# Start and late batches of a one-core Sinkhorn attention and FFN kernel: exps of two heads merged in the first batch, P of the first pair spread on its own, fillers only in idle banks, two planner costs changed

## The chip, the cores and the metric

The kernel runs on one core of a Trainium2 chip. The metric is the device time of one execution in microseconds (us). Before the change the median of three runs was 229.92 us (229.88 to 229.97). Most executions of a kernel agree within 0.3%. Each execution also reports the mean clock that TensorE was granted (1.0 is full speed). Runs well above the fastest of the same kernel are called slow and kept out of every comparison.

## The reference

```python
def _attn_ref(q, k, v, sort_net):            # B=4, H=8, S=768, D=64, 8 blocks of 96
    P = sort_net                             # [4, 8, 8, 8]
    for _ in range(5):                       # Sinkhorn
        P = np.exp(P - P.max(-1, keepdims=True))
        P = P / (P.sum(-1, keepdims=True) + 1e-09)
        P = P / (P.sum(-2, keepdims=True) + 1e-09)
    k_sorted = einsum('bhij,bhjcd->bhicd', P, k_b)   # blocks of k and v mixed by P
    v_sorted = einsum('bhij,bhjcd->bhicd', P, v_b)
    scores = scale * q_b @ k_sorted^T        # within each block of 96
    return softmax(scores) @ v_sorted

def _moe_ref(x, w_in, w_out):                # x [3072, 512], w_in [512, 2048], w_out [2048, 512]
    h = np.maximum(x @ w_in, 0.0)
    return h * h @ w_out                     # of the attention's result, reshaped to tokens
```

The FFN is most of the work. Its first 384 tokens need the first half of batch 0's attention, and everything before that is start-up.

## The kernel before

The order of instructions on each engine is fixed by a small list scheduler in Python. Every stage is entered with an estimated cost in us and the stages that it depends on. The scheduler fills TensorE (PE) with attention stages that are due and otherwise with FFN work.

```python
FIRST = ("K0 V0 k1 v1 S0 t0 S1 k2 V2 t1 A0 S2 K3 t2 A1 V3 X0 A2 S3 t3 x1 A3 X2 x3")
```

This is the order of the first half of batch 0. The digit is the unit (a pair of heads). K and V sort k and v with P. S makes the scores and their exp. T transposes the sorted v. A multiplies exp by v and divides by the row sums. X transposes the result for the FFN. A capital means that ScalarE copies the result out of PSUM, a small letter that VectorE does.

Buffers rotate in rings: `ps1` has one PSUM bank (transposes of v and of the result share it), `p2` has two tiles of two banks (scores and A), `psf` has three banks. Before the FFN starts, gaps that the plan foresees on PE are filled with matmuls on a tile of ones, all into `p2[0]`, so that PE stays busy:

```python
    def fill(us, wide=False):
        if wide:
            ...      # int(us / 0.33) matmuls of 512 columns into p2[0]
        else:
            for _ in range(int(us / 0.08)):
                nc.tensor.matmul(out=p2[0][:, 1, 384:512], lhsT=ones, rhs=ones,
                                 start=True, stop=True)
...
    for op in plan.run():
        if op.eng == "PE":
            started = started or op in plan.ffn
            if filled and not started and op.gap > 0.15:
                fill(op.gap, op.begin < 11 and op.gap > 0.5)
            filled = True
        op.fn(op.eng)
```

P comes out of the Sinkhorn steps, is transposed (`pT`), and is spread over the partitions by eight matmuls for all heads at once. VectorE multiplies it with a mask for the first two heads, and ScalarE copies it for the others:

```python
    pe = plan.add("PE", 0.3, p_spread, [op] + old)
    w0 = build_w(0, 2, None, pe)                  # VectorE reads pt_ps
    cp = plan.add("ACT", 0.37, ... copy(out=pt, in_=tiles["pt"]), [pe])   # ScalarE reads pt_ps
    rf.use(sf, pe, w0, cp)
```

The exps of one half of a unit are two instructions, one for each head, which also permute the queries:

```python
            for h in range(2):
                def ex(e, h=h, st=st, et=et_r[u.et[hf]]):
                    nc.scalar.activation(
                        out=et[:, h, 0:HS].rearrange("p (n c a) -> p n c a", c=C0, a=NA),
                        in_=st["p"][0:96, h, 0:HS].rearrange("p (n a c) -> p n c a", c=C0, a=NA),
                        func=AF.Exp, scale=scale)
```

In batches 2 and 3 the sort is done by small matmuls from `kb` and `vb` (function `s_nat`, entered with a PE cost of 0.2). `kn` and `qi` are copied into natural order and transposed by DMA into `kx` and `qT`. Scores are entered with a cost of 0.17 in every batch. An FFN unit of 384 tokens has 16 groups of four `hp` matmuls (0.65 us each), then 48 `op` matmuls.

The softmax here doesn't subtract the row's maximum and nothing guards it: scores larger than these inputs give would overflow.

## Time and profile before

| | before |
|---|---|
| time, us | 229.92 |
| span in the profile, us | 228.1 |
| PE busy, us (share) | 220.0 (96%) |
| P transposed on PE (`pT` starts), us | 11.56 |
| last A of the first half starts, us | 21.41 |
| first FFN matmul, us | 23.68 |
| `wtp`, the first stage of batch 2's attention on PE, us | 83.86 |
| start of the last block of 64 `hp` matmuls, us | 203.47 |

Read it from the end. The last block of `hp` and what follows have no gaps, so the time is decided by when that block starts. The stretch from 23.7 to 83.9 us is dense FFN and attention of batches 0 and 1. What can be moved is the start (0 to 23.7) and holes between 84 and 203.

The page's chain of the work that ended last, before the change, as shares of the span by engine:

```profile
PE 81%; ACT 6%; DVE 6%; DMA 4%; issue 2%; POOL 0%; ACTq 0%; DVEq 0%; POOLq 0%
```

PE holds 81% of the chain. The 12% of ScalarE (ACT) and VectorE (DVE), 27 us, are not all waits of PE: PE is idle for only 228.1 - 220.0 = 8.1 us of the span. Four more lines of the very beginning are used below (the timeline: start us, duration us, engine, line, operation; x is the count; in brackets the idle time before it and what ended it):

```profile
5.30 0.96 PE L338 MATMUL p<-ones 128*128 128x512 bf16 x2
6.73 0.76 PE L458 MATMUL qtp<-ident,qb 64*64 64x64 bf16 x36 [0.46 <-DMA qb<-in_q_dram]
...
1.49 1.52 POOL L253 DMA_DIRECT2D qb<-in_q_dram  x2
...
3.11 0.37 DVE L322 TENSOR_TENSOR p_sb<-p_sb,rs 32x64 f32<-32x64 f32 x1
```

### The profile page before, as it was taken

What the parts mean: (1) busy time and instruction counts of PE and PEld (TensorE: products, weight loads), DVE (VectorE), ACT (ScalarE), POOL (GpSimd) and SP (SyncE); (2) the same over time, 40 slices, a digit from 0 to 9 for tenths busy, and PEclk for the clock granted to TensorE, in tenths of its full rate; (3) what the DMA queues carried; (4) which work ended last, traced back from release to release, by engine and by line L of the source; (5) the groups of instructions that cost most, each with busy time, mean ns of one, the idle gap of its engine ahead of it and who ended that gap; (6) DMA issues with size and microseconds to landing.
All of it is one profiled execution on the core that took longest, in us unless ns stands there. A gap on an engine that the chain in (4) does not pass through costs nothing.

```text
span 228.1 us, 5299 instructions
## 1 busy us (share of the span) xinstructions
PE 220.0 (96%) x2152; PEld 125.2 (55%) x2165; DVE 106.0 (46%) x295; ACT 122.3 (54%) x260; POOL 27.1 (12%) x49
## 2 busy tenths in 40 slices
PE   8998999999999999999999999999999999999993
PEld 2576666546665645535665455445665455446552
DVE  5777677407676416630667027523664045005300
ACT  4655676317875328734866248535774177137421
POOL 8963322200003200000000000000000000000000
PEclk9999999999999999999999999999999999999999
DMA  5999999999922999599821341998732210110012
GB/s 60 201 203 207 207 207 204 203 223 249 195 50 26 122 238 205 131 156 265 188 37 35 83 126 25 164 226 196 98 53 53 92 47 3 46 55 37 0 49 92
DMA packets 42744, 28.83 MB, mean 126 GB/s; under 512 B 22752, under 2 KB 38368, under 8 KB 42720
## 3 DMA queue, kind: packets, MB, share of 16 engines
q0 software_dynamic: 13888, 13.63, 37.4%
q1 hardware_dynamic: 28832, 14.86, 30.0%
q8 instruction: 17, 0.28, 0.5%
q14 instruction: 7, 0.06, 0.1%
HBM read 28.89 MB, written 7.91 MB: 161 GB/s over the span
## 4 chain that ended last, share of the span: by engine, by line
PE 81%; ACT 6%; DVE 6%; DMA 4%; issue 2%; POOL 0%; ACTq 0%; DVEq 0%; POOLq 0%
PE op L823 34%; PE hp L795 30%; PE p L544 3%; DVE ao L727 3%; PE p L716 3%; ACT h L803 2%; ACT et L567 2%; DMA qb<-in_q_dram 2%; PE p L503 2%; PE qtp L458 2%; PE op L857 2%; PE vbp L583 1%; PE p L617 1%; DMA qT<-qi 1%; PE p L343 1%
## 5 line engine op out<-in xcount | busy, mean ns | idle before, releaser
L795 PE MATMUL hp<-xT,w_in_bf 128*128 128x384 bf16 x512 | 91.0, 326 | 0.0
L823 PE MATMUL op<-w_out_bf,h 128*128 128x512 bf16 x355 | 82.4, 379 | 0.7
L803 ACT ACTIVATE h<-hp 128x384 bf16<-128x384 f32 x128 | 61.5, 497 | 24.1 <-PE hp L795 19.3
L806 DVE TENSOR_TENSOR h<-h 128x384 bf16<-128x384 bf16 x128 | 44.2, 355 | 53.2 <-ACT h L803 52.4
L795 PEld LDWEIGHTS <-w_in_bf 128*128 128x128 bf16 x512 | 47.1, 98 | 30.1 <-issue 0.7
L823 PEld LDWEIGHTS <-h 128*128 128x128 bf16 x368 | 34.9, 98 | 39.7 <-issue 0.7
L184 ACT COPY ob<-op 128x512 f32<-128x512 f32 (+1 forms) x25 | 14.2, 569 | 56.8 <-PE op L823 54.3
L567 ACT ACTIVATE et<-p 96x384 bf16<-96x384 f32 x64 | 26.2, 489 | 5.5 <-PE p L544 5.5
L727 DVE TENSOR_TENSOR ao<-p,rec 96x512 bf16<-96x512 f32 x32 | 22.0, 687 | 1.1
L726 DVE RECIPROCAL rec<-p 96x8 f32<-96x8 f32 x32 | 6.4, 199 | 21.4 <-PE p L716 18.7
L716 PEld LDWEIGHTS <-et 96*128 96x128 bf16 x256 | 10.7, 97 | 2.9 <-issue 0.3
L253 POOL DMA_DIRECT2D qb<-in_q_dram x8 | 6.0, 755 | 32.8 <-PE qtp L458 25.6
L186 DVE COPY vs<-vbp 96x512 bf16<-96x512 bf16 (+1 forms) x12 | 6.1, 509 | 7.1 <-PE vbp L583 6.9
L253 POOL DMA_DIRECT2D vb<-in_v_dram x10 | 6.6, 659 | 6.4 <-DMA w_in_bf<-in_moe_w_in_dram 3.6
L253 POOL DMA_DIRECT2D kb<-in_k_dram x10 | 6.6, 659 | 6.2 <-DMA w_in_bf<-in_moe_w_in_dram 1.8
L184 ACT CAST ksT<-p 128x768 bf16<-128x768 f32 (+1 forms) x7 | 4.6, 663 | 3.3 <-PE p L503 3.3
L544 PEld LDWEIGHTS <-kx 64*128 64x128 bf16 x128 | 4.6, 155 | 2.8 <-issue 2.8
L716 PE MATMUL p<-vs,et 96*128 96x65 bf16 x128 | 6.0, 193 | 0.0
L716 PE MATMUL p<-vblk,et 96*128 96x65 bf16 x128 | 5.6, 193 | 0.1
L458 PEld LDWEIGHTS <-qb 64*64 64x64 bf16 (+1 forms) x144 | 3.5, 109 | 3.9 <-issue 1.9
L583 PE MATMUL vbp<-ident,vsT 128*128 128x128 bf16 x64 | 5.6, 220 | 0.0
L544 PE MATMUL p<-qT,kx 64*128 64x96 bf16 x128 | 5.6, 226 | 0.0
(81 smaller groups left out, 132.0 us busy)
## 6 DMA issues: line engine op xcount, KB each, us to landing
out_dram<-ob SPq DMA_DIRECT2D x23, 256.0 KB, 2.6
qb<-in_q_dram POOLq DMA_DIRECT2D x8, 384.0 KB, 16.7
vb<-in_v_dram POOLq DMA_DIRECT2D x6, 384.0 KB, 17.1
kb<-in_k_dram POOLq DMA_DIRECT2D x6, 384.0 KB, 17.0
w_in_bf<-in_moe_w_in_dram POOLq DMA_DIRECT2D x4, 512.0 KB, 12.4
w_out_bf<-in_moe_w_out_dram POOLq DMA_DIRECT2D x4, 512.0 KB, 17.7
v_way<-vn SPq DMA_DIRECT2D x4, 396.0 KB, 3.9
vblk<-v_way SPq DMA_DIRECT2D x4, 396.0 KB, 4.0
```

What stands on the lines that cost most here:

```text
L184: nc.scalar.copy(out=out, in_=in_)
L253: nc.gpsimd.dma_start(out=dst, in_=src)
L458: nc.tensor.transpose(out=t["p"][64 * h:64 * (h + 1), a, :], in_=qb[p0:p1, 2 * hp + h, D * a:D * (a + 1)], identity=ident[p0:p1, p0:p1])
L544: nc.tensor.matmul(out=scp[:, h, BLK * n:BLK * (n + 1)], lhsT=(u.ksT[64 * h:64 * (h + 1), hf, BLK * n:BLK * n + 128] if u.b < 2 else kx_r[ ...
L567: nc.scalar.activation(out=et[:, h, 0:HS].rearrange("p (n c a) -> p n c a", c=C0, a=NA), in_=st["p"][0:96, h, 0:HS].rearrange("p (n a c) - ...
L583: nc.tensor.transpose(out=vbp[:, n, :], in_=u.vsT[:, i // NQ, BLK * (i % NQ):BLK * (i % NQ) + 128], identity=ident)
L716: nc.tensor.matmul(out=oup[:, h, 66 * n:66 * n + D + 1], lhsT=et_r[u.et[hf]][:, h, BLK * n:BLK * n + 128], rhs=(u.vs[:, NQ * hf + n, h, 0: ...
L727: nc.vector.tensor_tensor(out=u.ao[:, n0:n0 + NQ, :, :].rearrange("p n e d -> p e n d"), in0=ov[:, :, :, 0:D], in1=rec[:, :, :, None].to_b ...
L795: nc.tensor.matmul(out=t["hp", nt][:, 0:HS], lhsT=w_in_bf[:, kc, 128 * nt:128 * (nt + 1)], rhs=xT[:, kc, t0:t0 + HS], start=(kc == 0), sto ...
L803: nc.scalar.activation(out=t["h1", nt], in_=t["hp", nt][:, 0:HS], func=AF.Relu)
L806: nc.vector.tensor_tensor(out=t["h2"][:, nt, :], in0=t["h1", nt], in1=t["h1", nt], op=ALU.mult)
L823: nc.tensor.matmul(out=t["op", mt], lhsT=t["h2"][:, nt, 128 * mt:128 * (mt + 1)], rhs=w_out_bf[:, nt, :], start=(nt == 0), stop=(nt == NT ...
```

## The change

The intent: the start of batch 0 waits for small copies and exps, so give P to the first pair sooner, merge two exps into one, move copies to the engine that has time, and keep filler matmuls out of banks that someone still reads. The diff also edits two planner costs.

```diff
-FIRST = ("K0 V0 k1 v1 S0 t0 S1 k2 V2 t1 A0 S2 K3 t2 A1 V3 X0 A2 S3 t3 x1 A3 X2 x3")
+FIRST = ("K0 V0 K1 v1 S0 t0 S1 k2 t1 A0 V2 S2 K3 t2 A1 V3 X0 A2 S3 t3 x1 A3 X2 x3")
...
+    def idle(self, t0, t1):
+        for slot, ops in enumerate(self.all):
+            if all(op.end <= t0 or op.begin >= t1 for op in ops):
+                return slot
...
-        nc.gpsimd.memset(kx[:, 128 * NA:], 0.0)
+        nc.vector.memset(kx[:, 128 * NA:], 0.0)
...
-    def fill(us, wide=False):
+    def fill(us, slot):          # into p2[slot]; wide matmuls wherever us > 0.5
...
-            out=pick, in_=ident.rearrange("p (j c) -> p j c", c=C0)[:, :, 0:4]), [cp])
+            out=pick, in_=ident.rearrange("p (j c) -> p j c", c=C0)[:, :, 0:4]), [x_done[0, HP - 1, 0]])
...
         def ev(e):               # qT of batch 0 is stored in natural order
+            if b == 0:
+                copy(e, qT.rearrange("p (i c a) -> p i c a", a=NA, c=C0)
+                     [:, p0 // C0:p1 // C0, :, :], src.rearrange("p a (i c) -> p i c a", c=C0))
...
-            pe = plan.add("PE", 0.17, mm, [u.k_op, u.q_op] + old, due, mode="row")
+            pe = plan.add("PE", 0.17 if u.b < 2 else 0.26, mm, [u.k_op, u.q_op] + old, due,
+                          mode="row")
...
+            if u.b == 0:
+                def ex(e, st=st, et=et_r[u.et[hf]]):
+                    nc.scalar.activation(out=et[:, :, 0:HS], in_=st["p"][0:96, :, 0:HS],
+                                         func=AF.Exp, scale=scale)
...
-            pe = plan.add("PE", 0.2, mm, [landed[b, t, HP * g, 0], built["t"]] + old, due,
+            pe = plan.add("PE", 0.15, mm, [landed[b, t, HP * g, 0], built["t"]] + old, due,
...
-    pe = plan.add("PE", 0.3, p_spread, [op] + old)
+    pe = plan.add("PE", 0.25, lambda e: p_spread(e, "pt_01", 2), [op] + old)
     w0 = build_w(0, 2, None, pe)
...
+    pe = plan.add("PE", 0.3, lambda e: p_spread(e, "pt_ps", NH), [op] + old)
+    cp = plan.add("ACT", 0.37, lambda e: nc.scalar.copy(out=pt, in_=tiles["pt_ps"]), [pe])
...
-            if filled and not started and op.gap > 0.15:
-                fill(op.gap, op.begin < 11 and op.gap > 0.5)
+            slot = r2.idle(op.begin - op.gap, op.begin)
+            if filled and not started and op.gap > 0.15 and slot is not None:
+                fill(op.gap, slot)
```

## The prediction

> **What bounds the kernel now.** I read the page first, then the PE's own timeline from the start to the first FFN matmul, then VectorE and ScalarE over the same stretch, then the chain of waits, and last the PE's timeline in the later batches. The page gives the frame (busy us, share of the span, instructions):
>
> ```profile
> PE 220.0 (96%) x2152; PEld 125.2 (55%) x2165; DVE 106.0 (46%) x295; ACT 122.3 (54%) x260; POOL 27.1 (12%) x49
> ```
>
> PE is the bound, but "busy" here includes filler matmuls on `ones` and drawn-out tails of waits. The first useful FFN matmul starts at 23.7 us, and from there PE has work almost without a break to 224.5. So every microsecond taken from the start, and every hole in PE later, should come off the end one for one. The start, PE alone (start us, us, what):
>
> ```profile
> 19.34 0.27 PE L343 MATMUL p<-ones 128*128 128x128 bf16 x2 [0.18 <-DVE ao L727]
> 19.55 0.34 PE L544 MATMUL p<-qT,ksT 64*128 64x96 bf16 x8
> 19.82 0.40 PE L583 MATMUL vbp<-ident,vsT 128*128 128x128 bf16 x4
> 20.85 0.55 PE L343 MATMUL p<-ones 128*128 128x128 bf16 x7 [0.63 <-ACT et L567]
> 21.23 0.34 PE L764 MATMUL xtp<-ident,ao 96*128 96x96 bf16 x4
> 21.41 0.41 PE L716 MATMUL p<-vs,et 96*128 96x65 bf16 x8
> ```
>
> L343 is a filler. It writes the same PSUM tile (p2_0) from which ScalarE is still reading the scores of unit 3, so it waits 0.63 us for those exps, and only then do its seven matmuls run, ahead of the useful L764 and L716. L716 is the last A of the first half (A = exp x V). From its start at 21.41 to the first FFN matmul at 23.74 lie a fixed 2.33 us: matmuls, reciprocal, division, transpose, copy.
>
> VectorE and ScalarE in the same stretch:
>
> ```profile
> 12.50 0.42 DVE L388 TENSOR_TENSOR w_all<-mask,pt_ps 128x256 bf16<-128x256 bf16 x1 [0.53 <-PE pt_ps L377]
> 12.95 0.37 ACT L886 CAST pt<-pt_ps 128x256 bf16<-128x256 f32 x1 [1.44 <-DVE w_all L388]
> 13.36 1.03 DVE L388 TENSOR_TENSOR w_all<-mask,pt 128x256 bf16<-128x256 bf16 x2 [0.44 <-ACT pt L886]
> 14.30 0.55 DVE L186 CAST ksT<-tp 128x384 bf16<-128x384 f32 x1
> ```
>
> The ScalarE copy of P waits for VectorE, although both only read pt_ps; then VectorE waits for the copy. After 13.36 VectorE has almost no idle time to 20.2. It is what paces units 1 to 3.
>
> The later holes, PE alone, batch 2 (batch 3 has the same at 140.7 and 171.5):
>
> ```profile
> 90.28 0.82 PE L795 MATMUL hp<-xT,w_in_bf 128*128 128x384 bf16 x4
> 91.31 0.55 PE L617 MATMUL p<-vb,w_t 32*32 32x384 bf16 x16 [0.20 <-ACT kn L184]
> ...
> 120.92 1.48 PE L795 MATMUL hp<-xT,w_in_bf 128*128 128x384 bf16 x8
> 122.23 0.89 PE L716 MATMUL p<-vblk,et 96*128 96x65 bf16 x16
> ```
>
> Undisturbed, 16 L617 take 0.31 us start to start and 16 L716 take 0.51; here they take 0.48 (after waiting) and 0.87. These matter because the diff also edits two costs by which the scheduler plans.
>
> **What the Trainium skill says.**
> - "ScalarE: Activation LUTs", What ACT_TABLE_LOAD costs: an ACTIVATE with immediate operands takes 186 ns + 0.833 ns per element, and neighbours overlap by about 93 ns. The trace agrees: 384 elements take 489 ns, two back to back 0.86 us, a 768-element copy 0.80 us.
> - "PSUM — Partial Sum Buffer", PSUM bank collisions raise a hardware error: two engines on one bank must be kept apart, reads included. The trace shows the price: the copy of P starts at 12.95, just after w_all's end at 12.92.
> - "TensorE: Matmul & The Clock Gate", Wait — 56ns, not 53.3ns?: matmuls do not start closer than about 25 ns, however few columns. Eight pt_ps matmuls of 32 columns take 0.36 us, one 0.175: (0.36 - 0.175) / 7 = 26 ns. So a spread of 2 columns costs what one of 32 does.
> - "SBUF — State Buffer", Who interferes with whom: a VectorE operation with two SBUF inputs and a GpSimd operation that reads SBUF exclude each other. The first Sinkhorn product takes 0.37 us beside the GpSimd select on ident (3.09 to 3.41), later ones 0.21.
>
> **The change part by part.**
>
> *Memsets off GpSimd.* Three memsets hold GpSimd from 0.74 to 1.49; the q loads and all behind them start 0.75 us earlier. q lands at about 5.95 instead of 6.7, but the warm-up holds PE to 6.26 in both. VectorE gets three memsets of about 0.13 us; it is idle from 1.73 to 2.64, so they are free. Ident comes sooner, so the sel copy no longer delays the second exp (4.39, against 4.28 by the usual 0.04 us hop), and the 0.37 us product can fall to 0.21. Sum: at most 0.11 + 0.16; I take 0.25.
>
> *P of the first pair alone.* pt_01 ends at 12.38 as before; the full spread follows by about 12.6, in another bank, so ScalarE copies P at about 12.7, not 12.95. The second w_all starts at 13.12 instead of 13.36: 0.24 for unit 1.
>
> *K1 to ScalarE, pick later.* VectorE loses a 0.55 us copy and one of 0.16. Against it ScalarE gets one of 0.48.
>
> *Merged exp.* 0.86 becomes 0.80 (186 + 0.833 x 768 = 826 ns; the copy of that size showed 0.80): 0.06 each on ScalarE, four of them before the FFN. The permutation moves to the qT copies, whose 384 elements stay. Alone this is nearly nothing.
>
> *Fillers.* The 2 + 2 + 7 fillers before A1, S3 and X1 vanish. X1 then waits for vs3, not for exp, and the filler.
>
> I walked the new order through with durations of before and a hop of 0.03 to 0.06 us (S scores, T transpose of V, A as above, X transpose of the result; all before the 0.25):
>
> ```
>               before   after
> A0 starts      16.29   15.75   vsT1, vs0 earlier on VectorE
> A1 starts      17.91   17.35   ao0 done at 17.28
> S3 starts      19.55   18.87   ao1 done at 18.80, no filler
> exp3 done      20.79   20.05
> vs3 done       20.68   20.14   VectorE, the later of the two
> A3 starts      21.41   20.38   X1 first, at 20.20
> FFN starts     23.74   22.71
> ```
>
> So 1.03 us, and with the 0.25 above, 1.28. w_in's first quarter lands at about 20.2 now (the GpSimd issue at 20.29 waited for it), 0.75 earlier after: no new wait. Batch 1's first k, v, q, issued from 20.3, land by about 44 and are used at 50.9: not bound.
>
> *Planner costs.* Scores of batches 2, 3 are entered at 0.26 instead of 0.17, and the small sort matmuls at 0.15 instead of 0.20. The built order shows what follows. Two hp groups (4 matmuls, 0.65 us each) instead of one stand between the k and v sorts; three instead of two between the S and A of unit 2; and A of unit 3 moves behind one hp and 8 op matmuls (0.65 + 8 x 0.217 = 2.39 us) instead of two hp (1.30). In batch 2 one VectorE copy of kn also moves ahead of a qi copy that waited 1.17 us for a DMA. Worth:
> - v sort: 91.79 less (90.28 + 0.65 + 0.31 = 91.24) = 0.55; about 0.45 in each batch, 0.9.
> - A of units 2 and 3: (0.61 - 0.51) + (0.87 - 0.51) = 0.46 per batch, 0.92. The four exps need 1.62 us, and 1.95 or 2.39 cover it.
> - The kn copy: PE spends 98.80 to 99.51 on 0.31 us of work; about 0.3, batch 2 only.
>
> Sum 2.1. With 1.28: 3.4 us. The walks assume that every hop stays typical; I take off about 0.4 for what I do not see. 229.92 - 3.0 = 226.9.
>
> **The rivals.**
> - *A new wait in the start.* K1's copy stands before exp0 on ScalarE and takes over from VectorE's slack: exp0 at 14.7 is only 0.04 us behind S0. If ScalarE lags there, A0 gains less. For: ScalarE is 1.9 of 2.0 us busy from 16 to 18. Against: it idles 0.72 before exp0 now. The start would give 0.6 instead of 1.28: 227.6.
> - *The late gain does not come.* Moving A later delays its norms and transposes, and the v rows go to memory 0.65 us later. For: DMA transposes stand on the chain at 95 to 98. Against: the next FFN unit starts 10 us after A3. Only the start counts: 228.7.
> - *PE cools without fillers.* The first ten wide fillers average 631 ns, the next seven 441, so PE's clock does step. Nineteen narrow fillers vanish after 17 us and two wide ones come: seven narrow ones in 0.55 us, less one latency of 0.22, are 55 ns each, so 1.05 us go and about 0.4 come, in 6 us with useful work around; unlikely. Were 10 us run at half speed, some 3 us would come back: about 230.
> - *Full gain.* No discount, and more alignment in batches 0 and 1: 226.0.
>
> **Range and chances.** The middle is 226.9; 228.3 allows for most of the late gain missing, 225.8 for a little more than the whole sum. Faster by over 2% needs 225.3 or less, 1.2 us beyond my full sum: 0.04. Slower by over 2% would take 4.6 us of new waits: 0.01. Within 2%: 0.95.
>
> **What would show it.** The first FFN matmul near 22.5; no filler waiting for an exp; P's copy on ScalarE near 12.5, beside w_all; the merged exp at 0.80. Later, the v sort following two hp groups without idle time, and 16 L716 taking 0.5 everywhere. I am wrong if the FFN starts after 23.1, if a pair of S and A still has a hole, or if the PE chain between 24 and 84 us, whose order does not change, lengthens.

## The result, and the profile after

The changed kernel took 226.47 us (median of 4 runs, 226.37 to 226.76), the kernel before 229.9 us in the same rounds (229.83 to 229.97). The ratio is 0.9853, with a 95% interval of 0.9836 to 0.987. A ratio here is the mean time of one kernel's fast runs over that of the other's fast runs of the same rounds, so it is not quite the ratio of the medians. The result lies within 2%, as predicted, and 0.4 us below the predicted 226.9.

| | before | predicted | after |
|---|---|---|---|
| time, us | 229.9 | 226.9 | 226.47 |
| A0 starts | 16.29 | 15.50 | 15.46 |
| A1 starts | 17.91 | 17.10 | 17.17 |
| S3 starts | 19.55 | 18.62 | 18.60 |
| `exp` of unit 3 done | 20.79 | 19.80 | 19.79 |
| `vs` of unit 3 done | 20.68 | 19.89 | 19.79 |
| A3 starts | 21.41 | 20.13 | 20.00 |
| FFN starts | 23.68 | 22.46 | 22.27 |
| `wtp` | 83.86 | | 82.45 |
| last block of 64 `hp` | 203.47 | | 200.09 |

(The predicted column is the walk of the prediction with its 0.25 us for the Sinkhorn steps taken off. Its times for the FFN's start are the chain's, which had 23.74 where the timeline has 23.68; on the timeline its 22.46 is 22.40.)

The page of the changed kernel, its busy times and its chain of the work that ended last:

```profile
PE 216.6 (97%) x2130; PEld 122.9 (55%) x2145; DVE 105.7 (47%) x297; ACT 122.1 (54%) x253; POOL 26.4 (12%) x46
...
PE 92%; DMA 2%; DVE 2%; ACT 1%; issue 1%; ACTq 0%; POOLq 0%
```

PE's share of the chain rose from 81% to 92%, and ScalarE and VectorE together fell from 12% to 3%. That is some 20 us, far more than the 3.4 us won, so it measures which path the chain was followed along, not waits that went. PE's idle time hardly moved (8.1 us before, 224.3 - 216.6 = 7.7 after). What fell by 3.4 us is the time drawn as busy: the fillers take 8.8 us instead of 11.5 (1.1 us of it is a shorter warm-up, which won nothing: PE waited for q instead), the v sorts of batches 2 and 3 2.0 instead of 2.4, the A there 5.3 instead of 5.6. The waits were drawn into those instructions.

The start, PE's timeline after the change:

```profile
18.60 0.35 PE L550 MATMUL p<-qT,ksT 64*128 64x96 bf16 x8 [0.18 <-DVE ao L742]
18.90 0.38 PE L598 MATMUL vbp<-ident,vsT 128*128 128x128 bf16 x4
19.84 0.33 PE L779 MATMUL xtp<-ident,ao 96*128 96x96 bf16 x4 [0.56 <-DVE vs L194]
20.00 0.42 PE L731 MATMUL p<-vs,et 96*128 96x65 bf16 x8
22.27 0.82 PE L810 MATMUL hp<-xT,w_in_bf 128*128 128x384 bf16 x4
```

No filler (L350 here) stands before S3 or before the X at 19.84. That X no longer waits for exps but, as the prediction said, for the `vs` copy. It shares the single bank of `ps1` with the transposed v. A3 follows 0.16 us later, and the FFN 2.27 us after A3, as before (21.41 to 23.68).

ScalarE and VectorE:

```profile
12.21 1.57 DVE L391 TENSOR_TENSOR w_all<-mask,pt 128x256 bf16<-128x256 bf16 x3 [0.52 <-PE pt L380]
12.35 0.37 ACT L905 CAST pt<-pt_ps 128x256 bf16<-128x256 f32 x1 [1.05 <-PE pt_ps L380]
18.98 0.81 ACT L573 ACTIVATE et<-p 96x768 bf16<-96x768 f32 x1
```

The copy of P now starts at 12.35, while VectorE is inside its first product, and the three products run without a break. The merged exp takes 0.81 us.

The beginning, on PE, GpSimd and VectorE:

```profile
1.06 4.11 PE L350 MATMUL p<-ones 128*128 128x512 bf16 x12 [1.06 <-DVE ones L213]
6.51 0.76 PE L461 MATMUL qtp<-ident,qb 64*64 64x64 bf16 x36 [1.34 <-DMA qb<-in_q_dram]
...
1.24 1.52 POOL L261 DMA_DIRECT2D qb<-in_q_dram  x2 [0.80 <-POOLq L1018]
...
3.15 0.21 DVE L330 TENSOR_TENSOR p_sb<-p_sb,rs 32x64 f32<-32x64 f32 x1
```

The q loads are issued only 0.25 us earlier (1.24 instead of 1.49), not 0.75, because GpSimd stands idle 0.80 us before its first DMA even with no memset there. PE's warm-up ends at 5.17, and PE then waits 1.34 us for q. The first product of the Sinkhorn steps takes 0.21 instead of 0.37 us.

Batch 2, PE:

```profile
88.88 1.47 PE L810 MATMUL hp<-xT,w_in_bf 128*128 128x384 bf16 x8
90.28 0.38 PE L632 MATMUL p<-vb,w_t 32*32 32x384 bf16 x16
...
96.96 0.60 PE L632 MATMUL p<-vb,w_t 32*32 32x384 bf16 x16
...
120.12 1.89 PE L838 MATMUL op<-w_out_bf,h 128*128 128x512 bf16 x7
121.84 0.66 PE L731 MATMUL p<-vblk,et 96*128 96x65 bf16 x16
```

Eight `hp` matmuls stand before the v sort at 90.28, which now takes 0.38 and waits for nothing. The 16 L731 of unit 3 take 0.66 as drawn and 0.50 from start to start. One hole is left in each of the two batches: the second v sort, here at 96.96, takes 0.60, because only four `op` matmuls lie between it and the k sort whose copies it waits for.

Where the time went, from these traces: the FFN starts 1.41 us earlier; `wtp` is also 1.41 us earlier, so the stretch from 24 to 84 us did not change; the first FFN matmul after batch 2 is 2.47 us earlier (133.45 to 130.98) and the one after batch 3 3.38 us (182.71 to 179.33). So batch 2 gave 2.47 - 1.41 = 1.06 us and batch 3 gave 3.38 - 2.47 = 0.91 us. The sum is 3.38 us, and the medians differ by 3.43.

### The profile page after: what moved, and what is told of

It is laid out like the page before. It is cut to its first block, busy times and chain, and to the rows that moved or that the text cites. A ratio compares the mean times of both kernels' runs of the same rounds, so it can differ in the third digit from the quotient of the medians.

```text
span 224.3 us, 5245 instructions
## 1 busy us (share of the span) xinstructions
PE 216.6 (97%) x2130; PEld 122.9 (55%) x2145; DVE 105.7 (47%) x297; ACT 122.1 (54%) x253; POOL 26.4 (12%) x46
## 4 chain that ended last, share of the span: by engine, by line
PE 92%; DMA 2%; DVE 2%; ACT 1%; issue 1%; ACTq 0%; POOLq 0%
PE hp L810 37%; PE op L838 35%; PE p L550 4%; PE p L731 3%; DMA qb<-in_q_dram 2%; PE p L510 2%; PE qtp L461 2%; PE vbp L598 2%; PE op L872 2%; PE p L350 1%; PE p L632 1%; PE xtp L779 1%; PE tp L510 1%; DVE ao L742 1%; ACT h L818 0%
## 5 line engine op out<-in xcount | busy, mean ns | idle before, releaser
L582 ACT ACTIVATE et<-p 96x384 bf16<-96x384 f32 x48 | 19.4, 491 | 2.4 <-PE p L550 2.4
L731 PEld LDWEIGHTS <-et 96*128 96x128 bf16 x256 | 10.6, 97 | 2.9
L350 PE MATMUL p<-ones 128*128 128x512 bf16 (+1 forms) x36 | 8.8, 360 | 1.1 <-DVE ones L213 1.1
L573 ACT ACTIVATE et<-p 96x768 bf16<-96x768 f32 x8 | 6.3, 802 | 2.1 <-PE p L550 2.0
L731 PE MATMUL p<-vs,et 96*128 96x65 bf16 x128 | 6.0, 193 | 0.0
L461 PE MATMUL qtp<-ident,qb 64*64 64x64 bf16 (+1 forms) x144 | 4.7, 204 | 1.3 <-DMA qb<-in_q_dram 1.3
```

The lines of the kernel that those rows point to most:

```text
L350: nc.tensor.matmul(out=out, lhsT=ones, rhs=rhs, start=True, stop=True)
L461: nc.tensor.transpose(out=t["p"][64 * h:64 * (h + 1), a, :], in_=qb[p0:p1, 2 * hp + h, D * a:D * (a + 1)], identity=ident[p0:p1, p0:p1])
L582: nc.scalar.activation(out=et[:, h, 0:HS].rearrange("p (n c a) -> p n c a", c=C0, a=NA), in_=st["p"][0:96, h, 0:HS].rearrange("p (n a c) - ...
L731: nc.tensor.matmul(out=oup[:, h, 66 * n:66 * n + D + 1], lhsT=et_r[u.et[hf]][:, h, BLK * n:BLK * n + 128], rhs=(u.vs[:, NQ * hf + n, h, 0: ...
```

## The experiments

Twelve kernels ran, all with correct results, three rounds each against the kernel before. Two numbers of each trace carry most of the verdicts: the first FFN matmul (22.27 in the changed kernel, 23.68 before) for the start, and the distance from `wtp` to the last block of `hp` for the late part (200.09 - 82.45 = 117.64 in the changed kernel, 203.47 - 83.86 = 119.61 before).

### Both planner costs undone

```diff
-            pe = plan.add("PE", 0.17 if u.b < 2 else 0.26, mm, [u.k_op, u.q_op] + old, due,
+            pe = plan.add("PE", 0.17, mm, [u.k_op, u.q_op] + old, due,
-            pe = plan.add("PE", 0.15, mm, [landed[b, t, HP * g, 0], built["t"]] + old, due,
+            pe = plan.add("PE", 0.2, mm, [landed[b, t, HP * g, 0], built["t"]] + old, due,
```

> The changed kernel with the two planner costs of batches 2 and 3 put back (scores 0.17, small sort 0.20); the instruction order of the first 84 us is that of the changed kernel. My theory: the late reordering is worth 1.97 us (1.06 in batch 2, 0.91 in batch 3, read from the two traces), so 226.47 + 1.97 = 228.4 us, first FFN matmul still at 22.3. Rival (everything came from the start, and the later holes only moved because the start moved): 226.5 us.

Measured: 228.47 us (228.22 to 228.5), ratio 0.9936 (0.9918 to 0.9954). From `wtp` to the last block it is 119.60 us, as before the change. PE's timeline shows the two holes of before again:

```profile
90.04 0.55 PE L632 MATMUL p<-vb,w_t 32*32 32x384 bf16 x16 [0.20 <-ACT kn L192]
...
120.94 0.89 PE L731 MATMUL p<-vblk,et 96*128 96x65 bf16 x16
```

Two numbers by which the planner sorts the stages, which change no instruction, are worth 2.0 of the 3.4 us.

### One planner cost undone at a time

The first kernel undoes only the cost of the late scores, the second only that of the small sort matmuls (the two halves of the diff above).

> The changed kernel with only the scores cost back at 0.17: A of units 2 and 3 stands behind two hp groups again. My theory: 0.45 us lost in each late batch, 226.47 + 0.9 = 227.4 us, and 16 L731 matmuls at some 0.87 us in the last unit of each batch. Rival (that hole is filled by other waits anyway): within 0.2 of 226.5.

Measured: 227.34 us (227.3 to 227.44), ratio 0.9891 (0.9875 to 0.9906). `wtp` to the last block 118.58: 0.94 us more than the changed kernel.

> The changed kernel with only the small sort's cost back at 0.20: one hp group instead of two between the k and v sorts, and in batch 2 the qi copy ahead of the kn copy on VectorE again. My theory: 0.43 + 0.45 for the v sorts and 0.18 for the kn copy, 226.47 + 1.06 = 227.5 us. Rival (only the scores cost matters): 226.5 us.

Measured: 227.49 us (227.44 to 227.76), ratio 0.9899 (0.9883 to 0.9914). 118.79: 1.15 us more. The scores' cost carries the A of units 2 and 3 (0.94), and the sort's cost the v sort and the `kn` copy (1.15). Their sum, 2.09, is near the 1.96 of both.

### Only the planner costs, on the kernel before

> The kernel before with nothing but the two planner costs changed; its first 84 us are in the order of before. My theory: 229.9 - 1.97 = 227.9 us, first FFN matmul still at 23.7. Rival (the late gain needs the earlier start, for example because the DMA transposes are then ready earlier): above 229 us.

Measured: 229.33 us (229.32 to 229.45), ratio 0.9978 (0.9962 to 0.9993). This missed: 0.6 us came of an expected 2, and the number fell where the rival had put it (above 229). Batch 2 gained what it should (48.52 us from `wtp` to the next unit, 49.59 before, 48.53 in the changed kernel). In batch 3 there was a new hole, first on PE, then on VectorE:

```profile
146.86 0.35 PE L617 MATMUL p<-vb,w_t 32*32 32x384 bf16 x8
148.52 0.35 PE L617 MATMUL p<-vb,w_t 32*32 32x384 bf16 x8 [1.30 <-DVE kn L186]
```

```profile
147.51 0.96 DVE L186 CAST kn<-p 128x768 bf16<-128x768 f32 x1 [2.67 <-DMA kx<-kn]
```

The second half of the v sort waits 1.30 us for the PSUM tile that the copy to `kn` reads. The copy waits 2.67 us for a `kn` buffer, which a transposing DMA (`kx<-kn`) still reads. That DMA, issued at 142.20, took 5.2 us from issue to landing. In the changed kernel the DMA of the same place (issued at 140.65) took 3.5 us, so the buffer was free in time. The instruction orders of the late part are the same in both kernels. In the kernel before it took 5.1 us (issued at 142.87), where no one waited for it. Over the traces, the transfer that follows the v rows' way to memory in batch 3 took 5.1 or 5.2 us in the three kernels with the old fillers (the kernel before, this one and the next) and 3.5 in ten with the new ones. One of the ten differs from the kernel before in nothing but the fillers ("Only the filler rule", below). So the shorter transfer goes with the earlier start, much as the rival said; why was not found.

### The same with a fourth kn buffer

```diff
-    rkx, rkn, rqi = Ring(3), Ring(3), Ring(2)
+    rkx, rkn, rqi = Ring(3), Ring(4), Ring(2)
-    ... name=f"kn{n}") for n in range(3)]
+    ... name=f"kn{n}") for n in range(4)]
```

> late_alone with four buffers for kn instead of three, the order of every engine unchanged. In late_alone a kn copy on VectorE waited for a transposing DMA still reading its buffer (5.2 us to landing, at other places 3.5) and held PE for 1.30 us in batch 3. My theory: that wait is all that late_alone lacked, so 229.33 - 1.30 = 228.0 us. Rival (the DMA delays something else next, or the gain of the order itself is small without the new start): above 229.0.

Measured: 227.95 us (227.9 to 227.99), ratio 0.9911 (0.9896 to 0.9926); `wtp` to the last block 117.67, as in the changed kernel. The DMA still took 5.2 us. The v sort of batch 3 waits for nothing now:

```profile
146.70 0.60 PE L617 MATMUL p<-vb,w_t 32*32 32x384 bf16 x16
```

So the buffer was all that the late part lacked. The changed kernel has three buffers and is spared this wait because the transfer is shorter there.

### Only the filler rule, on the kernel before

The diff is the change's `idle`, `fill` and the last lines of the loop, nothing else.

> The kernel before with nothing but the rule for fillers (only in an idle bank pair, with the new widths). My theory: the seven fillers that wait for the exps of unit 3 vanish, X1 starts at about 20.7 when vs3 is copied, A3 at about 20.8 instead of 21.41, so 0.6 us: 229.3 us. Rival (fillers only fill idle time and cost nothing): 229.9.

Measured: 229.03 us (229.01 to 229.05), ratio 0.9958 (0.9943 to 0.9973), 0.86 us faster than before where 0.6 was expected. PE's timeline:

```profile
17.77 0.41 PE L719 MATMUL p<-vs,et 96*128 96x65 bf16 x8
...
20.44 0.33 PE L767 MATMUL xtp<-ident,ao 96*128 96x96 bf16 x4 [0.56 <-DVE vs L194]
20.60 0.42 PE L719 MATMUL p<-vs,et 96*128 96x65 bf16 x8
...
22.87 0.82 PE L798 MATMUL hp<-xT,w_in_bf 128*128 128x384 bf16 x4
```

A1 starts 0.14 us earlier than before (17.91), A3 0.81 (21.41), the FFN 0.81 (23.68). The fillers that went, above all the seven at 20.85, gave more than half of the start's gain of 1.41.

### The changed kernel with one spread of P

```diff
-    pe = plan.add("PE", 0.25, lambda e: p_spread(e, "pt_01", 2), [op] + old)
+    pe = plan.add("PE", 0.3, lambda e: p_spread(e, "pt_ps", NH), [op] + old)
     w0 = build_w(0, 2, None, pe)         # reads pt_ps again
-    (second spread into its own bank)
```

> The changed kernel with one spread of P, which VectorE and ScalarE read one after the other again. My theory: ScalarE copies P 0.25 us later and the second w_all starts as much later, and the first half passes on 0.2 to 0.3 of it: 226.7 us. Rival (the path runs through K0 and V0, which do not need the copy): 226.5.

Measured: 227.0 us (226.73 to 227.66, a wider spread than usual, all at a clock of 1.0); ratio 0.9879 (0.986 to 0.9899). The spans of the four are 224.7 to 224.8 us, so the spread lies outside the span, and against the changed kernel's 224.3 to 224.6 the loss is 0.1 to 0.5. The profiled run (226.73) is what was expected. The first FFN matmul is at 22.64, 0.37 us later, while `pT` is where it was (11.30). ScalarE's line and PE's two show how:

```profile
12.69 0.37 ACT L902 CAST pt<-pt_ps 128x256 bf16<-128x256 f32 x1 [1.45 <-DVE w_all L391]
```

```profile
13.57 0.38 PE L510 MATMUL tp<-w_all,kb 128*64 128x64 bf16 x12 [0.20 <-DVE w_all L391]
...
14.09 0.38 PE L510 MATMUL tp<-w_all,vb 128*64 128x64 bf16 x12
```

The copy of P waits for VectorE again. K1 loses only 0.07 us by it (13.50 in the changed kernel), but V1 0.37 (13.72). A filler pair that stood before K1 in the changed kernel stands between K1 and V1 here. So of the 0.37 us some belongs to the spread and some to where the plan puts its fillers.

### The changed kernel with K1 and the pick copy on VectorE

```diff
-FIRST = ("K0 V0 K1 v1 S0 t0 S1 k2 t1 A0 V2 S2 ...
+FIRST = ("K0 V0 k1 v1 S0 t0 S1 k2 V2 t1 A0 S2 ...
-            out=pick, ...), [x_done[0, HP - 1, 0]])
+            out=pick, ...), [cp])
```

> The changed kernel with K1's copy and the pick copy back on VectorE at their old places in the order. My theory: VectorE paces units 1 to 3, so 0.71 us more on it before vs3 costs 0.3 to 0.7 us: 226.8 to 227.2. Rival (ScalarE's copy of K1 only moved the wait to exp0): 226.5 or less.

Measured: 226.57 us (226.39 to 226.75), ratio 0.9851 (0.9837 to 0.9866). My theory missed. The rival's number came, to within 0.07 us, but not its reason: exp0 starts at 14.42 in both kernels, right behind S0, so K1's copy holds it up on neither engine. PE's timeline:

```profile
15.70 0.42 PE L731 MATMUL p<-vs,et 96*128 96x65 bf16 x8
...
17.21 0.41 PE L731 MATMUL p<-vs,et 96*128 96x65 bf16 x8 [0.18 <-DVE ao L742]
```

A0 starts 0.24 us later (15.46 in the changed kernel), since V2's matmuls stand before it again, but A1 only 0.04 (17.17), and the FFN 0.04. With P split, VectorE has slack enough for the copies that were moved off it. The run moves K1, V2 and the pick copy together, so none of them is priced alone.

### The changed kernel with two exps again

```diff
             if u.b == 0:
-                def ex(e, st=st, et=et_r[u.et[hf]]): ...   # both heads
+                for h in range(2):
+                    def ex(e, h=h, st=st, et=et_r[u.et[hf]]):
+                        nc.scalar.activation(out=et[:, h, 0:HS], in_=st["p"][0:96, h, 0:HS],
+                                             func=AF.Exp, scale=scale)
```

> The changed kernel, but in batch 0 the exp of a half's two heads is two instructions again (instruction orders else the same). My theory, that the merged exp is worth next to nothing: 226.5 (226.4 to 226.6), first product of the FFN within 0.1 us of 22.27. Rival, that one exp instead of two is a real part of the gain of the start (it is the first thing the change names): 226.7 to 226.9, first product of the FFN at 22.5 or later.

Measured: 226.58 us (226.44 to 226.64), ratio 0.9856 (0.9841 to 0.9872). The four exps of units 0 and 1 take 1.62 us on ScalarE where the two merged ones take 1.50:

```profile
14.50 1.62 ACT L574 ACTIVATE et<-p 96x384 bf16<-96x384 f32 x4
```

S0 to A0 is 14.11 to 15.54 here and 14.03 to 15.46 in the changed kernel, 1.43 us in both. The first FFN matmul is at 22.34, 0.07 us later, but `pT` was already 0.08 later (11.37). The merged exp, the first thing that the change names, is worth nothing measurable.

### The changed kernel with kx zeroed on GpSimd

```diff
-        nc.vector.memset(kx[:, 128 * NA:], 0.0)
+        nc.gpsimd.memset(kx[:, 128 * NA:], 0.0)
```

> The changed kernel with the zeroing of kx back on GpSimd. My theory, that the zeroing delays the first spread of P by way of GpSimd: 226.7, P ready on TensorE at about 11.56 instead of 11.29, first product of the FFN at about 22.5. Rival, that the 0.27 us are absorbed by waits later in the start (as VectorE's K1 was): 226.5, first product of the FFN at 22.3.

Measured: 226.67 us (226.66 to 226.7), ratio 0.9861 (0.9846 to 0.9877). `pT` starts at 11.52 and the FFN at 22.45, each 0.2 us later. The first Sinkhorn product is long again:

```profile
3.15 0.33 DVE L330 TENSOR_TENSOR p_sb<-p_sb,rs 32x64 f32<-32x64 f32 x1
```

The last Sinkhorn product (`pf`) starts 0.23 us later (11.26, 11.03 in the changed kernel). But the first q transposes also start 0.22 us later (6.73 and 6.51). Both lead to `pT`. Over all fourteen traces, `pf` starts at 11.26 to 11.30 in the five kernels with this zeroing on GpSimd, and at 11.02 or 11.03 in eight of the nine with it on VectorE (11.16 in the other), so 0.23 us on the Sinkhorn way is shown. The step from `pf` to `pT` is not so steady: with the zeroing on VectorE `pT` starts at 11.29 or 11.30 in five traces and at 11.37 to 11.53 in four, three of which have `pf` at 11.03. In the run with only the scores' cost undone, whose start is that of the changed kernel, `pT` is at 11.48 and the FFN at 22.45, as in this run. So a difference of 0.2 us in `pT` or the FFN's start between two single traces proves little.

### The changed kernel without fillers after 11.5 us

```diff
-            if filled and not started and op.gap > 0.15 and slot is not None:
+            if filled and not started and op.gap > 0.15 and slot is not None and op.begin < 11.5:
```

> The changed kernel with no filler matmul after 11.5 us (those before, while the inputs are awaited, stay). My theory: with the fillers gone TensorE's granted clock stays at 1.0, as the gaps of the start are under 1.1 us each, and the time is 226.3 to 226.5. Rival, that the fillers are still needed: the clock of the start's slices falls below 1.0 and the time rises to 227 or more, up to 229.

Measured: 226.74, 226.3, 228.04 and 228.1 us (median 227.39), ratio 0.9896 (0.985 to 0.9943). The first two had a mean clock of 1.0, the other two of 0.992. This is unclear as a ratio and both theories are half right. In the profiled run (226.74, clock 1.0) the FFN starts 22.52 - 11.53 = 10.99 us after `pT`; in the changed kernel it is 22.27 - 11.29 = 10.98. So, with `pT` taken as the start, the fillers that the changed kernel has after it cost nothing on the path. But two of four executions were 1.55 us longer (the mean of 228.04 and 228.1 less that of the others) at a lower clock, while the 48 executions of the changed kernel and of the eleven other experiments all had 0.997 or more. The Trainium skill, "TensorE: Matmul & The Clock Gate", What's actually happening, has PE run at half its clock after at least one idle window of about 3.4 us, with windows that run freely. One such window would cost 3.4 / 2 = 1.7 us, an estimate from that page. That fits the 1.55, but no profile of those two executions exists, so that the start is where they lost it is not shown. Nor is it shown that the missing fillers were the cause: the kernel before, with all its fillers, twice ran at a mean clock of 0.971 and 4.4 us longer, in 25 executions. Two of four against none of 48 speaks for the fillers, but more executions and a profile of a slow one would be needed.

The same run shows something else, in the part of PE's timeline where no filler was removed:

```profile
11.00 0.61 PE L350 MATMUL p<-ones 128*128 128x512 bf16 x2
11.53 0.20 PE L374 MATMUL pT<-ident,pf 32*64 32x32 bf16 x1
```

`pf` was done at 11.24, as in the changed kernel, but `pT` starts only at 11.53, behind two wide fillers. The q loads had taken 5.5 us to land instead of 5.2, the q transposes and the fillers behind them were 0.3 us later, and the plan's order puts `pT` behind those. A filler in an idle bank still takes PE's time.

### The changed kernel with three additions

```diff
-            st["p"] = xtp = ps1.tile([128, u.ni, BLK], BF16, tag="p1", name="xtp")
+            (first half of batch 0:) xtp = psf.tile([128, u.ni, BLK], BF16, tag="pf", name="xtp")
-            op = plan.add(AD, cost_f(2 * NA * D), ev, [pe] + oldm)
+            op = plan.add(AD, (cost_f(2 * NA * D)[0] + 0.3, cost_f(2 * NA * D)[1] + 0.3), ev, [pe] + oldm)
-    rkx, rkn, rqi = Ring(3), Ring(3), Ring(2)
+    rkx, rkn, rqi = Ring(3), Ring(4), Ring(2)
```

> The changed kernel with three additions: the transposes of the first half's result take their banks from another ring than the one in which they now wait for a bank; the planner is told that the kn and vn copies cost 0.3 us more, so that two groups of op matmuls stand between the second sorts; and kn has four buffers. From the rows of the changed kernel: about 0.2 us in the start and 0.22 in each of batches 2 and 3, so 225.8. Rival: the start is held by the evictions and not by the bank, and the later order moves transposing DMAs so that another wait takes the place of the one removed: 226.4 or more.

Measured: 225.7 us (225.66 to 225.81), ratio 0.982 (0.9804 to 0.9835). That beats both kernels: 0.77 us below the changed kernel's 226.47 by the medians, each against the kernel before in its own rounds. PE's timeline:

```profile
19.11 0.34 PE L783 MATMUL xtp<-ident,ao 96*128 96x96 bf16 x4
19.84 0.43 PE L731 MATMUL p<-vs,et 96*128 96x65 bf16 x8 [0.40 <-ACT et L573]
...
22.06 0.82 PE L816 MATMUL hp<-xT,w_in_bf 128*128 128x384 bf16 x4
...
97.60 0.38 PE L632 MATMUL p<-vb,w_t 32*32 32x384 bf16 x16
```

The X that waited 0.56 us for the bank of `vs` runs at 19.11 in another ring. A3 starts at 19.84 and now waits for the exp; the FFN starts 0.21 us earlier. The second v sort of batch 2 has eight `op` matmuls before it and takes 0.38 instead of 0.60; `wtp` to the last block is 117.20, 0.44 us less. These two make 0.65 of the 0.77 us. The three additions were not run one by one.

## Why the prediction was right

**The sum was right and the discount was not needed.** The prediction's terms were 1.28 us for the start and 2.1 us for the late part, less 0.4 for what was not seen. Measured are 1.41 and 1.97, together 3.38. Nothing took the 0.4 back, and it is nearly all of the difference between 226.9 and 226.47.

**The start.** With its 0.25 us the walk holds to 0.07 us as far as `exp3`. The rest of the error, 0.13 us, comes after: `vs3` is 0.10 us earlier than walked and A3 0.13. The "fixed 2.33 us" from A3 to the FFN held, though the number mixed two views: on the timeline it is 2.27 us both before and after. The step that the prediction left without a number of its own, the fillers, is the largest: 0.81 us alone (22.87 for 23.68). The P split is 0.37 when undone, against 0.24 in the prediction for unit 1. The filler pair that changes its place is in that figure. The earlier `pT` is 0.27 (11.56 to 11.29). These three sum to 1.45, near the 1.41. They come from single traces and were taken from both ends (one added to the kernel before, one removed from the changed kernel), so the agreement is no proof that they simply add.

**The parts that were said to be nearly nothing.** The merged exp is 0.80 us, as expected, and worth nothing (S0 to A0 1.43 us with it and without). K1's move to ScalarE was not priced by itself; undone together with V2's and the pick copy's it costs 0.04 us, too little to tell from nothing. The prediction called VectorE what paces units 1 to 3. For the kernel before the trace agrees (from 13.36 to 20.68 its only drawn wait is 0.19 us), though no run moved the copies there; after the P split it has idle time there again (0.36 us before 14.14, 0.17 before 15.34).

**The step that failed.** "The q loads and all behind them start 0.75 us earlier. q lands at about 5.95 instead of 6.7": the loads start 0.25 us earlier, and the first q transpose, 0.22 earlier, is at 6.51. GpSimd waited 0.80 us before its first DMA with nothing in front of it. The prediction took this transfer for hidden behind the warm-up, which "holds PE to 6.26 in both"; here the warm-up ended at 5.17, and q's landing held PE, as it had in the kernel before (0.46 us). (The twelve warm-up matmuls take from 4.11 to 5.30 us over the traces, so in some it does reach 6.3.) In the profiled run of the kernel without late fillers, a landing 0.3 us later held up `pT` by 0.24 us, though `pf` was ready. The predicted 0.25 us came out (0.27), by the steps named for it: the sel copy ends sooner, so the second exp starts at 4.16 instead of 4.39, and the first product takes 0.21 instead of 0.37. That the q transposes came earlier by as much was needed too, as the traces read: their fillers ended just in time. There is luck in the 0.27: of the nine traces with this zeroing on VectorE, five have `pT` at 11.29 or 11.30 and four later, up to 11.53.

**The late part.** Batch by batch: the v sort gave 0.43 us in each (0.45 predicted), the A of units 2 and 3 0.45 in each (0.46), and the `kn` copy 0.18 rather than 0.3 in batch 2. That copy's v sort keeps a hole of 0.53 us from start to start for 0.31 us of work, since only four `op` matmuls stand before it. The experiments that undo one cost give 0.94 and 1.15 for the same terms.

**The rivals.** No new wait took over the start: exp0 starts at 14.42, while S0 ends at 14.38. PE did not cool: the clock is 1.0 in the profile and at least 0.997 in every run. In two of the four executions without late fillers the mean clock was 0.992, so this rival may have named a real danger that the remaining fillers avert; that is not shown. The rival that the late gain does not come was wrong for this kernel, but not far from coming true. On the kernel before, the same two costs gave 0.6 us instead of 2, by the `kn` buffer and a transfer of 5.2 us. The prediction did not see that its late term hangs on that transfer.

**What stays open:** why that transposing DMA takes 3.5 us to landing with the new fillers and 5.2 us with the old ones; where the two executions with a clock of 0.992 lost their time, and whether fillers would have saved it; and how the 0.37 us of the P split divide between the spread and the fillers' place.

## What to carry to other kernels

A filler is an instruction like any other: it waits for whoever reads its bank, and work behind it waits with it. So give it a bank that no one uses, and look in the timeline for fillers with a wait before them. In a planned schedule, the estimated costs by which the stages are sorted can be worth more than a merged instruction: here two of them gave 2.0 us and the merged exp none. Before pricing an instruction that gets shorter, ask who waits for it; and when a gain depends on a buffer coming free in time, try one buffer more, as a transfer that is short for a reason you don't know may be holding it.

## What the Trainium skill lacked or had wrong

- "DMA: Bandwidth & Descriptors" gives a bandwidth for the transpose by DMA but no time for a single small transposing transfer. Here 128 x 768 bf16 from SBUF to SBUF took 2.7 to 6.2 us from issue to landing, and the difference between 3.5 and 5.2 was worth 1.3 us of PE's time where a buffer hung on it.
- "TensorE: Matmul & The Clock Gate" tells of idle windows and busy windows, but not how busy a window must be to count as busy. In the run without late fillers the longest wait of PE from 11.6 to 22.6 us was 0.6 us, and PE was busy for 8.65 of these 11.0 us. That profiled execution kept its clock of 1.0; two of the other three had a mean clock of 0.992 (where in the execution is not known).
- "SBUF — State Buffer", Who interferes with whom, calls the ports that VectorE shares with GpSimd an exclusive lock, but does not say how much of a blocked operation is left when the lock is released. The product of 32 x 64 that starts at 3.11, 3.15, 3.17 or 3.24 us beside the select on GpSimd takes 0.37, 0.33, 0.31 or 0.24 us: it ends at 3.48 in all four, less than 0.1 us after the select's drawn end (3.39 to 3.41). One that starts at 3.32 takes 0.21. So the direction agrees, and the wait does not add the full 0.21 after the select; spans on GpSimd are drawn roughly.
- "ScalarE: Activation LUTs", What ACT_TABLE_LOAD costs: the formula gives 826 ns for 768 elements, and the merged exp took 802.
- No page that I know tells when GpSimd can issue its first DMA. Here it was at 1.24 us, after 0.80 us without any work, and a memset of 0.75 us before it delayed it by only 0.25.
